# Placing the stationary halves of g at 0 or 192 bytes modulo 256 in an attention and FFN kernel

## The chip, the cores and the metric

The kernel runs on one core of a Trainium2 chip. The metric is the device time of one execution in microseconds (us). The engines are named as the profile names them: PE is TensorE's matmul stream and PEld its loading of stationary operands, DVE is VectorE, ACT is ScalarE, POOL is GpSimd, and SP is SyncE, which issues the DMAs.

## The reference

A block-sparse attention feeds a feed-forward layer with a squared ReLU, all in float32:

```python
# q, k, v: [4, 8, 768, 64]; block 32, window 16
k_sum = k.reshape(B, H, nb, 32, D).max(axis=3)
v_sum = v.reshape(B, H, nb, 32, D).mean(axis=3)
scores = concat([where(|i - j| < 16, q @ k.T / 8, -1e9), q @ k_sum.T / 8 + log(32)])
x = softmax(scores) @ concat([v, v_sum])          # -> [3072, 512]
h = x @ w_in                                      # w_in [512, 2048]
r = maximum(h, 0)
g = s * (r * r) + b
out = g @ w_out                                   # w_out [2048, 512]
```

## The kernel before

The 3072 rows are worked in 12 chunks `c` of 256 rows (three for each batch). For each chunk the attention makes `x` transposed, split into an upper and a lower part (`xh`, `xl`, type float32r), and the feed-forward layer runs over 16 steps `f` of 128 hidden columns. Two steps make a pair `q`, so a chunk has pairs 0 to 7. Products are made from halves: a number is split into an upper half that float32r holds and the rest, and lower times upper, upper times lower and upper times upper are summed.

**`hidden`** (L460) makes a step's hidden values: 12 matmuls of 256 columns into `ph`, with a slice of `wh` or `wl` stationary and a slice of `xh` or `xl` moving. **`activate`** and **`scaled`** turn `ph` into `g` in a tile `r`, for two steps at once. **`upper_rows`** (tile `gh`, a CAST at L219 on DVE or a copy at L221 on ACT) and **`lower_rows`** (tile `gl`, L492 on DVE) split it. **`project`** (L504) multiplies: for each of the two 128-row blocks `t` of the chunk there are three matmuls of 512 columns into `po[c, t]`. There the g half is stationary (a slice of 128 columns, 512 bytes) and the output weights are moving (2048 bytes). `evict` copies `po` to SBUF and stores it.

The tiles lie in SBUF at addresses that the pools give. Of those that PE reads here, every slice of `wh` and `wl` starts at 0 bytes modulo 256, and every slice of `xh` and `xl` at 192. Before the change so do all slices of `gh` and `gl`: each name has four buffers of 2048 bytes, and a slice lies at a multiple of 512 from its buffer's start. A tile pool gives a new tile a buffer of its own name; the first instruction that writes it waits until the last readers of the buffer's former tile have ended. Engines run their instructions in the order of the program; the order is fixed by hand, so the change cannot move an instruction.

From chunk 3 on the order is regular: PE does four steps of `hidden`, then four of `project` (24 matmuls, first an even pair's twelve and then an odd pair's), with the next chunk's attention in between. Before that, `FIRST_ORDER` lists every call by a letter and numbers. Those that matter here are `H` (`hidden`), `J` (`activate`), `G` (`scaled`), `a` (`upper_rows`), `b` (`lower_rows`), `P` (`project`), `X` and `y` (`xh`, `xl` of a chunk), `S` (`scores`), and `O` (`evict`). A star moves the work to the other engine. Its last line and a half is

```python
"V2.3 G1.7* V2.1 X2.0 P0.14 y2.0 P0.15 X2.2 a1.7 y2.2 S3.2.0 S3.2.1 S3.0.0 S3.0.1 b1.7 O0.0 S3.3.0 S3.3.1 "
"O0.1* S3.1.0 S3.1.1 P1.11 b1.6"
```

after which come the exponentials of chunk 3 (`masked`, L323 on DVE, and `exps`, L336 on ACT), `hidden(2, 0)` and so on. There `a1.7` is the CAST to `gh` of chunk 1's pair 7 on DVE, `P0.15` is the last projection of chunk 0, and `P1.11` is the last that reads pair 5 of chunk 1. PSUM banks are shared too: `scores(3, 0)` writes the banks from which `y2.0` and `y2.2` read, and `hidden(2, 0)` writes a bank from which the masks of chunk 3's heads 2 and 3 read.

Of the kernel before, what the change touches and what calls it, by code (L numbers as in the profile page):

```python
# [11 lines left out]
F32 = mybir.dt.float32  # L12
F32R = mybir.dt.float32r
# [6 lines left out]
P = 128  # L20
# [9 lines left out]
T = NSUB * SUB  # L30
# [14 lines left out]
def windowed_attention_then_relu2_ffn(ctx, tc, qk, vwin, kt, vt, kq, vrow, wp, out):  # L45
# [8 lines left out]
    p2 = ctx.enter_context(tc.tile_pool(name="p2", bufs=2))  # L54
# [162 lines left out]
    def copy(by_dve, out_, in_):  # L217
        if by_dve:
            nc.vector.tensor_copy(out_, in_)  # L219
        else:  # L220
            nc.scalar.copy(out_, in_)  # L221
# [254 lines left out]
    def scaled(c, q, other=False):  # L476
# [3 lines left out]
        else:  # L480
            (nc.vector if other else nc.gpsimd).tensor_scalar(g, g, s_col, b_col, ALU.mult, ALU.add)  # L481

    def upper_rows(c, q, other=False):
        g = gg[c, q]
        gh = p2.tile([P, 2 * T], F32R, name="gh", bufs=4)
        copy(not other, gh, g)
        gg[c, q] = g, gh

    def lower_rows(c, q):
        g, gh = gg[c, q]  # L490
        gl = p2.tile([P, 2 * T], F32R, name="gl", bufs=4)
        nc.vector.tensor_tensor(gl, g, gh.bitcast(F32), ALU.subtract)  # L492
        gg[c, q] = gh, gl

# [52 lines left out]
    def of(fn, *more):  # L547
# [9 lines left out]
        "Ai": of(scale_weights, "in"), "Ao": of(scale_weights, "out"), "A": of(scale_weights, "both"),  # L557
        "Bi": of(convert_weights, "in"), "Bo": of(convert_weights, "out"), "D": of(convert_weights, "both"),
        "Y": hidden_part, "H": hidden, "J": activate, "G": scaled, "a": upper_rows, "b": lower_rows,
        "P": project, "O": evict, "h": upper_weights, "l": lower_weights,  # L560
    }
# [58 lines left out]
    for i in range(NF, NC * NF):  # L620
        c, f = divmod(i, NF)

        then(i - i % 4, HID, hidden, c, f)
        if f % 2:
            for stage_of in (activate, scaled, upper_rows, lower_rows):
                then(i, CHAIN, stage_of, c, f // 2)
        then((i + 4) | 3, PROJ, project, c, f)
        if f == NF - 1:
            for t in range(T // P):
                then((i + 4) | 3, EVICT, evict, c, t)  # L630
# [60 lines left out]
```

## Time and profile before

| | |
|---|---|
| median of 3 runs (lowest to highest) | 610.86 us (609.92 to 611.22) |
| profiled execution | 609.99 us, span 608.3 us |
| granted TensorE clock | 1.000 |
| PE busy | 597.9 us (98%) |
| DVE, ACT, POOL busy | 418.8, 276.3, 140.2 us |
| bytes moved by DMA | 66.41 MB |

The span runs from the first to the last instruction of the program; what lies around it is 1.7 us of the profiled execution's time. A matmul's recorded length includes its way through the array, so that matmuls overlap in the records. The pace of PE is read from start to start.

### The profile page before, as it was taken

The page shows a single profiled execution, that of the slowest core. Times are in us where ns is not written, and L with a number is a line of the kernel's source. Part 1 is how long each engine was busy: PE and PEld are TensorE (multiplying, and loading weights), DVE is VectorE, ACT ScalarE, POOL GpSimd, SP SyncE. Part 2 cuts the span into 40 slices and gives each one's busy share as a digit, 9 for nine tenths or more (in the row PEclk, how much of TensorE's full clock was granted, in tenths as well). Part 3 has the DMA queues.
Part 4 walks back from the last instruction along what each step waited for, and adds up shares of the span by engine and source line. Part 5 has one row for each costly group of instructions (what it writes and reads, how often), then busy time and mean ns, then how long its engine had stood idle before and what let it go on. Part 6 is the DMA issues. An engine that isn't in the chain of part 4 may idle for free.

```text
span 608.3 us, 13522 instructions
## 1 busy us (share of the span) xinstructions
PE 597.9 (98%) x5240; PEld 539.2 (89%) x5240; DVE 418.8 (69%) x1126; ACT 276.3 (45%) x712; POOL 140.2 (23%) x275
## 2 busy tenths in 40 slices
PE   7999999999999999999999999999999999999997
PEld 6798999899889998999999899999998998899896
DVE  6999997789489368668758748847848927832211
ACT  5999998262352262263154244235235236223221
POOL 4421012211511411412141411331141151141110
PEclk9999999999999999999999999999999999999999
DMA  8998713026205016103503211600710500200000
GB/s 340 398 400 359 283 71 113 13 93 158 103 3 186 1 45 226 57 20 105 171 20 102 86 45 56 227 18 16 221 60 1 187 9 11 87 1 1 36 1 35
DMA packets 26993, 66.41 MB, mean 109 GB/s; under 512 B 3824, under 2 KB 3824, under 8 KB 26928
## 3 DMA queue, kind: packets, MB, share of 16 engines
q1 hardware_dynamic: 26928, 65.54, 30.5%
q8 instruction: 41, 0.67, 0.4%
q14 instruction: 24, 0.20, 0.1%
HBM read 59.09 MB, written 6.29 MB: 107 GB/s over the span
## 4 chain that ended last, share of the span: by engine, by line
PE 88%; DVE 4%; ACT 3%; DMA 2%; issue 1%; SPq 1%; POOL 0%; POOLq 0%; ACTq 0%; DVEq 0%
PE po L504 41%; PE ph L460 39%; PE pav L417 4%; PE ps L301 3%; ACT pr L336 2%; DVE pT L368 2%; DMA wraw<-in_wp_dram 1%; DMA vsum<-vmean 1%; DVE pr L346 1%; PE pt L379 1%; DVE gl L492 1%; SPq L180 0%; POOL vw L263 0%; PE ph L441 0%; SPq L240 0%
## 5 line engine op out<-in xcount | busy, mean ns | idle before, releaser
L481 POOL TENSOR_SCALAR r<-r,sb_col 128x512 f32<-128x512 f32 x85 | 69.9, 822 | 384.7 <-ACT r L474 234.6
L504 PE MATMUL po<-wh,gh 128*128 128x512 f32 x384 | 151.3, 394 | 0.0
L504 PE MATMUL po<-wh,gl 128*128 128x512 f32 x384 | 150.7, 393 | 0.0
L504 PE MATMUL po<-wl,gh 128*128 128x512 f32 x384 | 150.5, 392 | 0.0
L468 ACT ACTIVATE r<-ph 128x512 f32<-128x512 f32 x93 | 55.4, 596 | 198.8 <-PE ph L460 158.4
L219 DVE CAST gh<-r 128x512 fp32r<-128x512 f32 x88 | 38.1, 433 | 133.4 <-POOL r L481 132.4
L368 DVE STREAM_TRANSPOSE pT<-pr 32x256 f32<-32x256 f32 x288 | 125.5, 436 | 4.1
L460 PE MATMUL ph<-xh,wl 128*128 128x256 f32 x760 | 118.5, 278 | 0.0
L460 PE MATMUL ph<-xl,wh 128*128 128x256 f32 x760 | 117.3, 276 | 0.0
L460 PE MATMUL ph<-xh,wh 128*128 128x256 f32 x760 | 117.1, 276 | 0.0
L460 PEld LDWEIGHTS ph<-xh,wl 128*128 128x128 f32 x760 | 104.5, 188 | 5.1 <-DVE wl L144 0.2
L460 PEld LDWEIGHTS ph<-xl,wh 128*128 128x128 f32 x760 | 101.0, 188 | 0.0
L460 PEld LDWEIGHTS ph<-xh,wh 128*128 128x128 f32 x760 | 100.3, 188 | 0.0
L504 PEld LDWEIGHTS po<-wh,gl 128*128 128x128 f32 x384 | 72.1, 188 | 15.2 <-issue 1.0
L504 PEld LDWEIGHTS po<-wh,gh 128*128 128x128 f32 x384 | 72.2, 188 | 14.6
L504 PEld LDWEIGHTS po<-wl,gh 128*128 128x128 f32 x384 | 72.1, 188 | 14.3
L336 ACT ACTIVATE pr<-pr,mn 128x120 f32<-128x120 f32 x176 | 66.9, 383 | 23.2 <-DVE mn L323 23.1
L492 DVE TENSOR_TENSOR gl<-r,gh 128x512 fp32r<-128x512 f32 x96 | 69.6, 725 | 3.8 <-ACT gh L221 1.0
L474 ACT ACTIVATE r<-r 128x512 f32<-128x512 f32 x92 | 58.2, 633 | 5.8 <-DVE r L470 2.9
L263 POOL COPY vw<-vsum 24x256 f32<-24x256 f32 x88 | 47.1, 568 | 35.7 <-DMA vsum<-vmean 21.9
L221 ACT COPY o<-po 128x512 f32<-128x512 f32 x23 | 13.5, 587 | 45.8 <-PE po L504 44.7
L346 DVE TENSOR_TENSOR pr<-pr,rs 128x480 f32<-128x480 f32 x48 | 32.5, 676 | 2.4 <-ACT pr L336 0.5
(88 smaller groups left out, 483.0 us busy)
## 6 DMA issues: line engine op xcount, KB each, us to landing
wraw<-in_wp_dram SPq DMA_DIRECT2D x32, 512.0 KB
qk<-in_qk_dram SPq DMA_DIRECT2D x44, 369.0 KB
vw<-in_vwin_dram SPq DMA_DIRECT2D x48, 256.0 KB
out_dram<-o SPq DMA_DIRECT2D x24, 256.0 KB
kraw<-in_kt_dram SPq DMA_DIRECT2D x12, 384.0 KB
vraw<-in_vt_dram SPq DMA_DIRECT2D x12, 252.0 KB
kq<-in_kq_dram SPq DMA_DIRECT2D x4, 512.0 KB
vraw<-in_vt_dram SPq DMA_DIRECT2D x6, 264.0 KB
```

What stands on the lines that cost most here:

```text
L219: nc.vector.tensor_copy(out_, in_)
L263: nc.gpsimd.tensor_copy(vw_t[c, p][WIN:KR, e], vsum[bi][WIN : WIN + NB, 2 * p + e, :].unsqueeze(1).to_broadcast([NB, NSUB, D]),)
L336: nc.scalar.activation(pr, pr, AF.Exp, bias=mn_of[c, p][:, n : n + 1], scale=-1.0, accum_out=sm_of[c, p][:, n : n + 1])
L346: nc.vector.tensor_tensor(pr, pr, rs.unsqueeze(2).to_broadcast([P, 4, KR]), ALU.mult)
L368: nc.vector.transpose(to[BLOCK * k : BLOCK * (k + 1), :, rows], src)
L417: nc.tensor.matmul(oi, vw[:KR, e, i, :], pi[:KR], start=True, stop=True)
L460: nc.tensor.matmul(ph, w[:, kc * P : (kc + 1) * P], x[:, kc], start=(n == 0), stop=(n == len(terms) - 1))
L468: nc.scalar.activation(r, ph, AF.Relu)
L474: nc.scalar.activation(r, r, AF.Square)
L481: (nc.vector if other else nc.gpsimd).tensor_scalar(g, g, s_col, b_col, ALU.mult, ALU.add)
L492: nc.vector.tensor_tensor(gl, g, gh.bitcast(F32), ALU.subtract)
L504: nc.tensor.matmul(po[c, t], a[:, t * P : (t + 1) * P], w[:, 512:], start=(f == 0 and n == 0), stop=(f == NF - 1 and n == len(terms) - 1),)
```

## The change

The halves get two names each, `gha` and `ghb`, `gla` and `glb`, with two buffers each. In chunks 2 to 11 an even pair uses b and an odd pair a; in chunks 0 and 1 it is the other way round. A small tile `gap` (two buffers of 32 bytes) is put between the a buffers and the b buffers, so that a slices lie at 192 bytes modulo 256, as before, and b slices at 0. What lies behind them moves up by 64 bytes: `vhalf`, `vmean`, `qk` and `vw`. All of the rest stays where it was.

```diff
+    def half_name(name, c, q):
+
+        return name + "ba"[(q + (c < 2)) % 2]
+
     def upper_rows(c, q, other=False):
         g = gg[c, q]
-        gh = p2.tile([P, 2 * T], F32R, name="gh", bufs=4)
+        gh = p2.tile([P, 2 * T], F32R, name=half_name("gh", c, q), bufs=2)
         copy(not other, gh, g)
         gg[c, q] = g, gh
 
     def lower_rows(c, q):
         g, gh = gg[c, q]
-        gl = p2.tile([P, 2 * T], F32R, name="gl", bufs=4)
+        gl = p2.tile([P, 2 * T], F32R, name=half_name("gl", c, q), bufs=2)
+        if (c, q) == (0, 0):
+            p2.tile([P, 8], F32, name="gap")
         nc.vector.tensor_tensor(gl, g, gh.bitcast(F32), ALU.subtract)
         gg[c, q] = gh, gl
```

The instructions and their order are the same on every engine. What differs is which earlier reader some instructions wait for. The one place where that waits for a much later reader is DVE's `a1.7`. Before, its buffer was one that had long been read. With two buffers for each name the odd pairs of chunks 0 and 1 share two: one is held by pair 5 of chunk 1 until `P1.11`, which comes later, so `a1.7` takes that of pair 7 of chunk 0, which `P0.15` reads. DVE there before:

```order
L433 TENSOR_TENSOR xl_1745<-pav_1710,xh_1737 128x512 [waits Activation_49]
L219 CAST gh_1754<-r_1707 128x512 [waits DVE_49]
L433 TENSOR_TENSOR xl_1745<-pav_1696,xh_1737 128x512 [waits Activation_49]
L492 TENSOR_TENSOR gl_1777<-r_1707,gh_1754 128x512 [waits DVE_49]
L219 COPY o_1790<-po_847 128x512 [waits PE_49]
L492 TENSOR_TENSOR gl_1807<-r_1683,gh_1705 128x512
L323 ISA pr_1809,mn_1811<-ps_1757,mask_first_90 128x120 [waits PE_49]
```

and after (the rows are `y2.0`, `a1.7`, `y2.2`, `b1.7`, the copy of `O0.1*`, `b1.6` and the first mask of chunk 3):

```order
L433 TENSOR_TENSOR xl_1746<-pav_1711,xh_1738 128x512 [waits Activation_49]
L219 CAST ghb_1755<-r_1708 128x512 [waits DVE_49,PE_49]
L433 TENSOR_TENSOR xl_1746<-pav_1697,xh_1738 128x512 [waits Activation_49]
L498 TENSOR_TENSOR glb_1778<-r_1708,ghb_1755 128x512 [waits DVE_49]
L219 COPY o_1791<-po_848 128x512
L498 TENSOR_TENSOR gla_1808<-r_1684,gha_1706 128x512
L323 ISA pr_1810,mn_1812<-ps_1758,mask_first_90 128x120 [waits PE_49]
```

The wait for PE moved from the copy to the CAST, three instructions earlier, and it is for the same matmul: the last of `P0.15`. PE's part that depends on these rows, after the change:

```order
L301 MATMUL ps_1768<-qk_1049 64x120 [waits DVE_49,Pool_49]
L301 MATMUL ps_1768<-qk_1049 64x120
L301 MATMUL ps_1769<-qk_1049 64x120 [waits DVE_49]
...
L510 MATMUL po_897<-wh_1258,ghb_1587 128x512
L460 MATMUL ph_1854<-xh_1738,wl_443 128x256 [waits DVE_49,PE_49,Activation_49]
```

The third row waits for `y2.2`, the last for the mask that reads its bank last; both waits stand there before the change too.

## The prediction

> **What bounds the kernel now.** I read the page's head first, then the chain that ended last.
>
> ```profile
> span 608.3 us, 13522 instructions
> PE 597.9 (98%) x5240; PEld 539.2 (89%) x5240; DVE 418.8 (69%) x1126; ACT 276.3 (45%) x712; POOL 140.2 (23%) x275
> PE 88%; DVE 4%; ACT 3%; DMA 2%; issue 1%; SPq 1%; POOL 0%; POOLq 0%; ACTq 0%; DVEq 0%
> ```
>
> PE carries 88% of the chain at 98% busy, so a change of its pace counts almost everywhere. The 4% of DVE and 3% of ACT are where it does not. The same chain in order of time, from 100 to 180 us, shows where they are:
>
> ```profile
> 117.44 2.97 PE po L504 x12
> 120.41 1.40 PE ps L301 x48
> 121.84 0.28 DVE pr L323
> 122.16 4.43 ACT pr L336 x23
> ...
> 153.09 3.55 DMA vsum<-vmean
> ...
> 163.20 1.47 POOL vw L263 x2
> 164.72 1.61 PE pav L417 x46
> ```
>
> From 120.4 to 164.7 us the end is set by another line of work: chunk 3's masks on DVE, its exponentials on ACT, its normalizing and turning on DVE among the work of chunk 2, the block sums, their DMA, POOL's copies, and only then PE. The loads of PE's stationary operands show that PE really waits there:
>
> ```profile
> 162.07 0.80 PEld L417 LDWEIGHTS pav<-pT,vw 120*64 120x64 f32 x16
> 163.91 0.19 PEld L417 LDWEIGHTS pav<-pT,vw 120*64 120x64 f32 x2 [1.05 <-POOL vw L263]
> 164.72 1.47 PEld L417 LDWEIGHTS pav<-pT,vw 120*64 120x64 f32 x46 [0.62 <-POOL vw L263]
> ```
>
> The change touches this chain at its beginning, and PE's pace outside it. These are the two terms.
>
> **Term one: `a1.7` waits for `P0.15`.** The rows of PE, ACT and DVE around it, from the timeline before:
>
> ```profile
> 119.33 0.39 PE L504 MATMUL po<-wh,gh 128*128 128x512 f32 x1
> 120.02 0.40 PE L504 MATMUL po<-wh,gh 128*128 128x512 f32 x1
> 120.34 1.87 PE L301 MATMUL ps<-qk 64*64 64x120 f32 x64
> 123.63 0.28 PE L460 MATMUL ph<-xh,wl 128*128 128x256 f32 x1
> 119.76 0.59 ACT L221 COPY o<-po 128x512 f32<-128x512 f32 x1 [1.19 <-PE po L504]
> 118.72 0.42 DVE L219 CAST gh<-r 128x512 fp32r<-128x512 f32 x1
> 119.05 0.68 DVE L433 TENSOR_TENSOR xl<-pav,xh 128x512 fp32r<-128x512 f32 x1
> 119.65 0.68 DVE L492 TENSOR_TENSOR gl<-r,gh 128x512 fp32r<-128x512 f32 x1
> 120.45 0.69 DVE L219 COPY o<-po 128x512 f32<-128x512 f32 x1
> 121.06 0.68 DVE L492 TENSOR_TENSOR gl<-r,gh 128x512 fp32r<-128x512 f32 x1
> 121.84 0.28 DVE L323 CUSTOM_DVE_ANT_0 pr<-ps,mask_first 128x120 f32<-128x120 f32 x1
> 123.26 0.08 DVE L323 DVE_READ_ACCUMULATOR2_ANT mn<- 128x1 f32 x1
> ```
>
> ACT's copy of the first row block starts 0.43 us after the start of that block's last matmul (119.76 after 119.33), and DVE's copy of the second also 0.43 us after (120.45 after 120.02). So the end of `P0.15` is seen at 120.45, and that is when the CAST can start, instead of at 118.72. Behind it on DVE everything waits in order: `y2.2` 0.33 us later at 120.78 (the step of the rows above), `b1.7` 0.60 later at 121.38, the copy 0.60 later at 121.98, since its own wait is then over, `b1.6` 0.61 later at 122.59, and the first mask 0.60 to 0.78 later, at 123.19 to 123.37. It stood at 121.84: 1.35 to 1.53 us late. The least that could be recovered is nothing, which leaves the CAST's own 1.73 us. I take 1.4, since the 0.78 before the mask can hold a wait for PE's scores that is over by then; 1.35 and 1.73 are the ends.
>
> On PE this shows at two places. The second bank of `scores(3, 0)`, due a good quarter into the 1.87 us from 120.34, waits for `y2.2`, which ends at 121.46 instead of 119.73: some 0.6 us. `hidden(2, 0)` waits for the read-out of the seventh mask, at 123.34 before and about 124.75 now, and stood at 123.63: PE is then 1.1 to 1.2 us late. That lateness costs nothing more: at 162.07 plus 1.2 PE is still ahead of POOL, which lets it go on at 164.72. But POOL's end is the chain from the mask, whose links are work on DVE and ACT in order, SP's issue and a DMA that follows them; I see no idle time in it to take up 1.4 us. So PE goes on at 166.1, and all later work is PE's. A gain is excluded here, since nothing starts earlier. The other waits that changed are for matmuls that ended long before. Term one: +1.4.
>
> **Term two: b slices at 0.** How fast PE streams, from its timeline (starts), and how often:
>
> ```profile
> 295.87 0.62 PE L460 MATMUL ph<-xl,wh 128*128 128x256 f32 x4
> 296.32 0.62 PE L460 MATMUL ph<-xh,wh 128*128 128x256 f32 x4
> 296.78 0.39 PE L504 MATMUL po<-wh,gl 128*128 128x512 f32 x1
> ...
> 301.35 0.39 PE L504 MATMUL po<-wh,gh 128*128 128x512 f32 x1
> 301.58 0.39 PE L504 MATMUL po<-wh,gl 128*128 128x512 f32 x1
> ...
> 302.04 0.39 PE L504 MATMUL po<-wh,gh 128*128 128x512 f32 x1
> 302.27 0.64 PE L460 MATMUL ph<-xh,wl 128*128 128x256 f32 x4
> 302.74 0.62 PE L460 MATMUL ph<-xl,wh 128*128 128x256 f32 x4
> ...
> 303.66 0.62 PE L460 MATMUL ph<-xh,wl 128*128 128x256 f32 x4
> ...
> 305.02 0.62 PE L460 MATMUL ph<-xh,wl 128*128 128x256 f32 x4
> ```
>
> the warm-up at the start,
>
> ```profile
> 8.25 0.63 PE L199 MATMUL warm<-ident 128*128 128x128 f32 x2
> 10.38 0.63 PE L199 MATMUL warm<-ident 128*128 128x128 f32 x2
> ```
>
> and the groups of the product `wh`, `gh` after 168 us, from 35 to 99.8 and from 99.8 to 120.4:
>
> ```profile
> L504 PE MATMUL po<-wh,gh 128*128 128x512 f32 x304 | 119.7, 394 | 0.0
> L504 PE MATMUL po<-wh,gh 128*128 128x512 f32 x40 | 15.8, 394 | 0.0
> L504 PE MATMUL po<-wh,gh 128*128 128x512 f32 x14 | 5.5, 395 | 0.0
> ```
>
> The 24 projections from 296.78 to 302.27 take 228.8 ns each. `hidden`'s settled pace (12 matmuls from 303.66 to 305.02) is 113.3 ns for 256 columns, so 226.7 for 512. The warm-up matmuls at the start, ten from 8.25 to 10.38, take 213 ns for four passes over 128 columns. So a projection is stretched by something, and the address of the stationary slice could be part of it. The last three rows count one of the three products in the stretches where PE is the chain: 3 x 358 = 1074 projections, of which about half, 537, read b slices.
>
> What the trace has on the address: while a projection (moving at 0) runs, the next stationary slice is loaded. That is a g slice at 192, save under the last of the 24, where it is a slice of `wl` at 0. This one takes 0.23 us (302.04 to 302.27) as the one at 301.35 does. Under the last `hidden` matmul (moving at 192) the slice is `gl` at 192 instead of a weight at 0, and that group of four takes 0.46 us (296.32 to 296.78) as the one before does 0.45. Both combinations show no effect, so I take 0.
>
> Its ends: at most the whole stretch goes, 228.8 - 213 = 15.8 ns, times 537 = 8.5 us of gain. At worst each load disturbs the stream as in the first group after a projection, 0.47 us for four where settled ones take 0.453: 4.2 ns a load, 2.3 us of loss. The shift of `qk` and `vw` by 64 bytes I put at 0: `scores` reads both operands from one tile, so their relation stays, and a load for `values` is half as long as one of g's.
>
> Here the Trainium skill speaks on both sides, and this hangs on nothing above. Its page "SBUF — State Buffer", section "Who interferes with whom", gives PE two independent read ports and says that PE never waits on anyone; by that the sum has no second term. Its page "TensorE: Matmul & The Clock Gate", section "Back-to-back issue gap", puts an isolated matmul of N columns at N/2.4 + 2.5 ns, 215.8 for 512; this trace disagrees by 13 ns. If placing at 0 brought that pace, an estimate by that page would be 7.0 us of gain in term two, a case inside the faster rival below.
>
> **Sum.** +1.4 + 0 on the profiled 609.99 gives 611.4. That run lies 0.87 below the median of the runs shown, 610.86, so I forecast 612.3. A measurement of this kernel tells about 0.2% (1.2 us) from no change.
>
> **Rivals.**
> - Faster: the load of a slice at 192 does disturb a stream that starts at 0, and at 0 it does not. For it speaks that the stretch is there and that it is larger in `project` than in `hidden`, whose two addresses differ the other way; against it the two rows above. It decides from (1.4 + 1.2)/537 = 4.9 ns a matmul, and reaches to 15.8: 609.6 down to 603.8 us, in the middle 606.7.
> - No change: the b projections fall to `hidden`'s pace, 2.1 ns each, 1.1 us in all, which pays most of the wait: 611.1 us. The small excess over 226.7 is a loss of step that a new address may end.
> - Slower still: two streams from 0 meet, 4.2 ns a load: 614.6 us. The rows against it are the same.
> - The wait costs nothing, because some link between 121.8 and 164.7 has slack that I don't see, and addresses do nothing: 610.9 us.
>
> **Chances.** Forecast 0.34 (own range 611.6 to 613.2, from the ends of term one and the scatter of the runs; some 0.10 of it lies within 0.2%), faster 0.32, no change by pace 0.18, slower still 0.11, free wait 0.05. Faster is 0.32; within 0.2% is 0.10 + 0.17 + 0.05 = 0.32; slower is 0.24 + 0.11 + 0.01 = 0.36. The range from 606.0 to 614.8 leaves out the lowest 2.2 of the 5.8 us of the faster case, 0.12, and about half of the slowest, 0.05.
>
> **What would show it.** In the profile after: `a1.7`'s CAST directly behind the end of `P0.15`, with `y2.2` and the masks late by some 1.4 us; `hidden(2, 0)` late by over a microsecond; PE let go by POOL at about 166.1. Then in a run of 24 projections the first 12 against the last 12: equal paces near 228.8 ns would confirm that the address does nothing. I am wrong if the first 12 take 224 or less, or 231 or more, each, or if the last 12 change as well, because the two halves of a run set each other's step.

## The result, and the profile after

The changed kernel takes 617.84 us (median of 4 runs, 617.14 to 618.7), the kernel before, on the same chip, 610.39 us (609.36 to 611.22). The ratio is 1.0124, with a 95% interval of 1.0102 to 1.0145: slower by some 7.5 us, where 612.3 was forecast. Two outlying executions, 3384.58 us of the kernel before and 1529.09 us of the kernel with `x` at 128 below, are in no ratio here, and the latter kernel's median is that of its other three. The page's head after:

```profile
span 616.3 us, 13522 instructions
PE 604.9 (98%) x5240; PEld 546.5 (89%) x5240; DVE 418.6 (68%) x1126; ACT 276.2 (45%) x712; POOL 138.5 (22%) x275
PE 87%; DVE 5%; ACT 3%; DMA 3%; issue 1%; SPq 1%; POOL 0%; POOLq 0%; DVEq 0%; ACTq 0%
```

The instructions are as many as before; PE is busy 7.0 us longer, and DVE's and DMA's shares of the chain are a point higher. The chain in order of time, around the stretch that PE does not set:

```profile
118.30 2.96 PE po L510 x12
121.28 0.43 DVE ghb L219
121.71 0.60 DVE xl L433
122.31 0.60 DVE glb L498
122.91 0.60 DVE o L219
123.51 0.60 DVE gla L498
...
165.75 1.47 POOL vw L263 x2
167.27 1.61 PE pav L417 x46
```

Where it went from `P0.15` directly to the scores, it now goes through the late CAST and the four instructions queued behind it on DVE. Between its two ends on PE lie 46.0 us (121.28 to 167.27), where 44.3 lay before (120.41 to 164.72). With the stretch ahead (35 us to `P0.15`'s end: 86.3 and 85.4) and the one behind (to the end of the span: 449.0 and 443.6), the 8.0 us between the two profiled spans are 0.9 + 1.7 + 5.4, in that order.

The largest part lies where nothing was to happen. The windows view from some microseconds after POOL lets PE go, for the matmuls of one line at a time (columns: window, its length, PE busy, PEld busy, granted clock, DMA share, GB/s): `hidden` before and after, then `project` before and after.

```profile
168.00:608.00 440.00, 202.66 (x1728) 202.15 (x1728) 1.00 0.21 70
170.50:616.00 445.50, 209.38 (x1728) 208.67 (x1728) 1.00 0.21 69
168.00:608.30 440.30, 215.81 (x912) 168.54 (x912) 1.00 0.21 70
170.50:616.30 445.80, 214.94 (x912) 168.56 (x912) 1.00 0.21 69
```

The projections, half of which now read b slices, gained 0.87 us. `hidden`, whose operands stand where they stood, lost 6.72 us, at the same granted clock (the attention's `values`, 0.4 us shorter, make up the rest of the 5.4). PE's timeline shows it matmul by matmul, through one run of 24 projections and the `hidden` behind it:

```profile
230.39 0.39 PE L510 MATMUL po<-wh,glb 128*128 128x512 f32 x1
...
232.88 0.39 PE L510 MATMUL po<-wh,ghb 128*128 128x512 f32 x1
233.11 0.39 PE L510 MATMUL po<-wh,gla 128*128 128x512 f32 x1
...
235.63 0.39 PE L510 MATMUL po<-wh,gha 128*128 128x512 f32 x1
235.86 0.63 PE L460 MATMUL ph<-xh,wl 128*128 128x256 f32 x4
236.33 0.63 PE L460 MATMUL ph<-xl,wh 128*128 128x256 f32 x4
...
241.04 0.64 PE L460 MATMUL ph<-xh,wh 128*128 128x256 f32 x4
241.51 0.39 PE L510 MATMUL po<-wh,glb 128*128 128x512 f32 x1
```

The twelve b projections take 230.39 to 233.11, 226.7 ns each; the twelve a, 233.11 to 235.86, 229.2. The ten groups of four from 236.33 to 241.04 take 0.471 us each, 117.8 ns a matmul. Before, `hidden` ran at 113.3.

### The profile page after: what moved, and what is told of

It reads as the page before. It is cut to its first block, busy times and chain, and to the rows that moved or that the text cites. A ratio compares the mean times of both kernels' runs of the same rounds, so it can differ in the third digit from the quotient of the medians.

```text
span 616.3 us, 13522 instructions
## 1 busy us (share of the span) xinstructions
PE 604.9 (98%) x5240; PEld 546.5 (89%) x5240; DVE 418.6 (68%) x1126; ACT 276.2 (45%) x712; POOL 138.5 (22%) x275
## 4 chain that ended last, share of the span: by engine, by line
PE 87%; DVE 5%; ACT 3%; DMA 3%; issue 1%; SPq 1%; POOL 0%; POOLq 0%; DVEq 0%; ACTq 0%
PE po L510 40%; PE ph L460 39%; PE pav L417 3%; PE ps L301 3%; ACT pr L336 2%; DVE pT L368 2%; DMA wraw<-in_wp_dram 1%; DMA vsum<-vmean 1%; PE pt L379 1%; SPq L180 1%; DMA kq<-in_kq_dram 1%; POOL vw L263 0%; DVE pr L346 0%; DVE ksum L156 0%; DVE glb L498 0%
## 5 line engine op out<-in xcount | busy, mean ns | idle before, releaser
L219 DVE CAST ghb<-r 128x512 fp32r<-128x512 f32 x43 | 18.5, 430 | 95.4 <-POOL r L481 93.6
L510 PE MATMUL po<-wh,glb 128*128 128x512 f32 x192 | 76.0, 396 | 0.0
L510 PE MATMUL po<-wl,gha 128*128 128x512 f32 x192 | 75.6, 394 | 0.0
L510 PE MATMUL po<-wh,gla 128*128 128x512 f32 x192 | 75.4, 393 | 0.0
L510 PE MATMUL po<-wl,ghb 128*128 128x512 f32 x192 | 74.8, 390 | 0.0
L510 PE MATMUL po<-wh,ghb 128*128 128x512 f32 x192 | 74.7, 389 | 0.0
L510 PE MATMUL po<-wh,gha 128*128 128x512 f32 x192 | 74.7, 389 | 0.0
L219 DVE CAST gha<-r 128x512 fp32r<-128x512 f32 x45 | 19.2, 427 | 45.9 <-POOL r L481 45.3
L510 PEld LDWEIGHTS po<-wh,gha 128*128 128x128 f32 x192 | 36.0, 188 | 8.0
L510 PEld LDWEIGHTS po<-wh,gla 128*128 128x128 f32 x192 | 36.0, 188 | 7.7
```

Source lines behind the costliest of these rows:

```text
L510: nc.tensor.matmul(po[c, t], a[:, t * P : (t + 1) * P], w[:, 512:], start=(f == 0 and n == 0), stop=(f == NF - 1 and n == len(terms) - 1),)
```

## The experiments

The timeline prints 10 ns; the trace's records hold single nanoseconds, and from them come the steps below (start to start). In the kernel before, a run of 24 at 192 goes 226, 229, 232 ns over and over (the three-step), and 231 lies, as a rule, between its last projection and the first `hidden` matmul. I call that interval the entry step. After it come five uneven `hidden` steps (118, 116, 118, 122, 119), and then 113.3 to the end of the group: `hidden` settles. In the changed kernel the b half goes 226, 227, 227; the three-step begins with the first a slice, the entry step is 226 or 227, and `hidden` never leaves 117.8. The theory from this: **the entry step decides `hidden`'s pace**, and the slices at 0 do harm only by shifting it. The rival: **placement**, that slices at 0 in the run before unsettle `hidden` by themselves.

Ratios are against the kernel before on the same chip, with 95% intervals. The kernel before has medians from 611.9 to 612.09 us beside the experiments, against 610.39 beside the changed kernel, so times of different rounds are better compared by their ratios.

**The wait alone.** The changed kernel without the gap tile: all halves at 192, the late CAST kept.

```diff
-        if (c, q) == (0, 0):
-            p2.tile([P, 8], F32, name="gap")
```

> The change without the small gap tile: two names with two buffers each, all slices of g at 192 as before. It keeps the late wait of a1.7 and nothing else. Entry theory (hidden settles at 113.3 ns or stays near 117.8 ns a matmul according to the step on which the projections before it end) and placement theory (slices of g at 0, or the tiles behind them moved by 64 bytes, slow hidden by themselves) both expect hidden at 113.3 ns and projections at 228.9 ns. The wait alone then costs 1.4 us: 611.8 us against 610.4. If the wait is free, 610.4.

612.58 us, ratio 1.0018 (1.0003 to 1.0033), 1.1 us. DVE's timeline and the chain:

```profile
120.76 0.43 DVE L219 CAST ghb<-r 128x512 fp32r<-128x512 f32 x1 [1.65 <-PE po L508]
123.50 0.28 DVE L323 CUSTOM_DVE_ANT_0 pr<-ps,mask_first 128x120 f32<-128x120 f32 x1
166.37 1.61 PE pav L417 x46
```

`P0.15` ends 0.31 us later here than before, the first mask comes 1.66 us later (121.84 before) and PE's release 1.65 (164.72). So the wait itself costs 1.35 us at the mask, and the chain behind it hands this on whole. `hidden` settles in 32 of 36 groups; the other four were entered on 226 or 227.

**The halves mixed, without the wait.** Chunks 0 and 1 take the two names by turns, so that `a1.7` finds a free buffer.

```diff
+    made = {"gh": 0, "gl": 0}
     def half_name(name, c, q):
-        return name + "ba"[(q + (c < 2)) % 2]
+        made[name] += 1
+        return name + ("ab"[(made[name] - 1) % 2] if c < 2 else "ba"[q % 2])
```

> The change with the names in chunks 0 and 1 given by turns instead of by pair, so that every buffer is reused after four pairs as before and a1.7 waits for nothing late; from chunk 2 on the places are those of the change. Both theories expect hidden near 117.8 ns from chunk 2 on. It should be 1.4 us below the changed kernel, about 616.4 us, with PE going on after the block sums some 1.4 us earlier than in the changed kernel (167.3 us).

616.55 us, ratio 1.0069 (1.0052 to 1.0085). The CAST starts at 120.35 without waiting, and `hidden` runs at 117.8 in all 36 groups (entry 226 or 227). More than half of the loss, 0.69% of 1.24%, is there without the wait. PE goes on behind POOL at 166.48, 0.79 us before the changed kernel where 1.4 was expected, mostly since `P0.15` itself ends 0.74 later here (122.02 against 121.28).

**All halves at 0**, from the kernel before; and **only the tiles behind the halves moved** by 64 bytes (`vhalf`, `vmean`, `qk`, `vw`).

```diff
+        if (c, q) == (0, 0):
+            p2.tile([P, 8], F32, name="gap")       # ahead of gh; in the second kernel behind gl
```

> The kernel before with a gap of 64 bytes ahead of g: four buffers each, all slices of g at 0. Entry theory: projections settle at 226.7 ns in both halves, end on 226 to 227, and hidden enters on the bad step: 117.8 ns. Against the changed kernel that is no wait (-1.4) and 2.2 ns less for the other half of the projections (-1.2): about 615.2 us. Placement theory: twice as many slices at 0 slow hidden more, 120 ns or more a matmul: about 622 us.

> The kernel before with the gap of 64 bytes behind g: g stays at 192 in four buffers, and only vhalf, vmean, qk and vw move, as in the change. Entry theory: hidden at 113.3 ns, 610.4 us, no difference. If the moved tiles were what slows hidden: 117.8 ns and about 616 us.

With all at 0: 615.7 us, ratio 1.0057 (1.0042 to 1.0072); every projection at 226.7 in the steady part, entry 226 or 227, `hidden` at 117.8 in all groups. Twice the slices at 0 do no more harm than half of them, which is what the entry step says. With only the rest moved: 611.37 us, ratio 0.9987 (0.9962 to 1.0012), entry 230 or more, `hidden` settled. Moving `qk` and `vw` costs nothing that shows.

**The halves swapped**: even pairs at 192 and odd at 0, so that the run ends on slices at 0.

```diff
-        return name + "ba"[(q + (c < 2)) % 2]
+        return name + "ba"[(q + 1) % 2]
```

> The change with the places swapped from chunk 2 on: even pairs at 192 and odd pairs at 0, so that a run begins at 192 and ends at 0. Chunks 0 and 1 and the late wait are as in the change. Entry theory: projections at 0 end on 226 or 227 ns, so hidden enters on the bad step: 117.8 ns, and the first matmuls at 192 are slower after an unsettled hidden (235 to 237 ns, as at 68.6 us of the changed kernel): 618 us, no better than the change. Placement theory: as the change, 617.8 us. A time near 611 us would speak against both.

619.01 us, ratio 1.0113 (1.0072 to 1.0153): entry 226 or 227, `hidden` at 117.8 throughout.

**One a projection fewer** in the changed kernel, so that a run is twelve b and eleven a; and **two fewer** in the kernel before, with nothing at 0.

```diff
         for t in range(T // P):
             for n, (a, w) in enumerate(terms):
+                if c > 1 and f % 4 == 3 and t == 1 and n == 0:     # second kernel: n < 2
+                    continue
```

> The changed kernel, with the product of the lower half left out for the second row block of the last step in each run of projections from chunk 2 on (its output lacks that small term): a run is 23 matmuls, 12 with slices at 0 and 11 at 192. All addresses are those of the changed kernel. Entry theory: the 11th matmul at 192 is the one of 231 ns, so hidden enters on the step on which it settles: 118, 116, 118, 122, 119 and then 113.3 ns. Saved: 40 runs x 0.23 us = 9.2, and some 1750 matmuls x 4.4 ns = 7.5 us: 617.8 - 16.7, about 601 us. Placement theory (slices at 0, or the moved tiles, slow hidden by themselves): hidden stays at 117.8 ns, 608.6 us.

> The kernel before, all slices at 192, with two products left out at the end of each run from chunk 2 on (lower times upper and upper times lower of the second row block in the last step; the output lacks these terms): a run is 22 matmuls. Entry theory: the 22nd is one of 226 ns, so hidden enters on the bad step and stays near 117.8 ns although nothing lies at 0: 610.4 - 40 x 0.46 + 8, about 600 us. Placement theory: hidden settles at 113.3 ns as before, 592 us.

Eleven a steps: the entry step is 230 or 231 and `hidden` settles in all 36 groups, with half of the slices at 0. The time, 606.73 us (one run, as for the next kernel), missed the entry theory's by 5.7 us. A part of it is that the shorter run lets PE catch up with POOL, for which PE now waits five times (before: twice, 1.4 us). From start to start, from 35 us on and against the changed kernel, `hidden` is 7.4 us shorter, as expected, and the projections 7.9 instead of 9.2; the attention's `values` take 2.8 us longer and its `scores` 1.0.

```profile
PE pav L417 <- POOL vw L263: 2.7, 5, 0.9
```

With 22 steps at 192 the groups alternate, with two breaks, 18 of each kind: entered on 226 or 227 they stay at 117.8; the three-step behind such a group begins elsewhere, the next entry is 231 to 236, and that one settles. The time, 599.42 us, is near the 600 expected by luck: the 600 has all groups slow, and with half of them slow the same sum gives 596. Two neighbouring groups on PE's timeline, in fours:

```profile
222.25 0.63 PE L460 MATMUL ph<-xl,wh 128*128 128x256 f32 x4
...
225.55 0.64 PE L460 MATMUL ph<-xh,wh 128*128 128x256 f32 x4
...
232.01 0.62 PE L460 MATMUL ph<-xh,wh 128*128 128x256 f32 x4
...
236.09 0.62 PE L460 MATMUL ph<-xh,wh 128*128 128x256 f32 x4
```

Seven fours in 3.30 us are 117.9 ns a matmul, nine in 4.08 are 113.3. So `hidden` is slow with nothing at 0 and fast with half at 0: placement alone is refuted. Both kernels leave work out, though, which the last pair mends.

**Other places**, looked for because a place at which `hidden` settles from any entry would beat both kernels. From the kernel before: `x` and g at 0; `x` at 128 or 64 and g at 0; g at 64 and `x` at 192.

```diff
+            if c == 0:
+                p2.tile([P, 8], F32, name="gap")            # ahead of xh: x and g at 0
...
-                prs_of[c, p // 2] = p2.tile([P, 8 * KR + 32], F32, name="pr", bufs=2)
+                prs_of[c, p // 2] = p2.tile([P, 8 * KR + 8], F32, name="pr", bufs=2)
+            if c == 0:
+                p2.tile([P, 16], F32, name="gapx")          # x at 128; with 8: x at 64
+        if (c, q) == (0, 0):
+            p2.tile([P, 16], F32, name="gap")               # with 24 for x at 64; g at 0
...
+        if (c, q) == (0, 0):
+            p2.tile([P, 16], F32, name="gap")               # g at 64, x at 192
```

> The kernel before with a gap of 64 bytes ahead of xh: all slices of x and of g at 0, where the weights are. If a stream settles from any entry when moving and stationary operand start at the same place modulo 256 (as the projections at 0 do), then hidden does too: 113.3 ns throughout, projections 226.7 ns, and the five slow matmuls at each entry (26 ns, some 46 times) go as well: 610.4 - 2.4 - 1.2, about 606.8 us. If it is the place of g that slows hidden: as all slices of g at 0, 615 us or more.

> The kernel before, with 64 bytes ahead of xh and 64 ahead of gh (pr is 96 bytes smaller to make room): x at 128 modulo 256, all g slices at 0. Entry theory without any part for x's place: projections at 226.7, so hidden is entered on 226 or 227 and stays at 117.8: 615.7 us as with x at 192. If x's place sets hidden's pace from whatever entry: 113.3 gives 609 to 610 us, 120.0 as with x at 0 gives 620 to 621 us.

> As the last, with x at 64 modulo 256 and all g slices at 0. Entry theory without any part for x's place: hidden at 117.8, 615.7 us. If x's place sets hidden's pace: 113.3 gives 609 to 610 us, 120.0 gives 620 to 621 us.

> The kernel before, with all g slices at 64 modulo 256 and x at 192. If only the place 192 brings the three-step: projections at 226.7 and hidden at 117.8, 615.7 us. If the three-step comes with any place but 0: the projections at 228.9, entry on 231, hidden settled, 611.4 us, the time of the kernel before.

| | median us | ratio (95%) | `project`, steady ns | entry ns | `hidden` ns |
|---|---|---|---|---|---|
| x 0, g 0 | 621.11 | 1.0145 (1.0127 to 1.0163) | 226.7 | 226, 227 | 120.0 |
| x 128, g 0 | 621.63 | 1.0167 (1.0142 to 1.0191) | 226.7 | 227 | 119.9 |
| x 64, g 0 | 616.40 | 1.0075 (1.0053 to 1.0097) | 226.7 | 226, 227 | 117.8 |
| x 192, g 64 | 618.15 | 1.0107 (1.0083 to 1.0132) | 233 | 229 to 236 | 113.3 or 117.8 |

None gains. `hidden` from `x` at 0, by PE's timeline:

```profile
188.11 0.64 PE L462 MATMUL ph<-xh,wh 128*128 128x256 f32 x4
188.59 0.64 PE L462 MATMUL ph<-xh,wl 128*128 128x256 f32 x4
189.07 0.64 PE L462 MATMUL ph<-xl,wh 128*128 128x256 f32 x4
189.55 0.64 PE L462 MATMUL ph<-xh,wh 128*128 128x256 f32 x4
```

0.48 us for four, 120 ns a matmul: equal addresses of the two operands, which go with the fastest `project`, go with one of the two slowest paces of `hidden`, no better than `x` at 128. As every entry in the first three rows is 226 or 227, they don't show what another entry would do there. With g at 64, which I expected to take the pace of 0 or of 192, `project` has a pace of its own, some 231 and 236 by turns; its entries of 235 or 236 (18 groups) settle, those of 229 or 230 (18 groups) don't.

**The order alone.** First g in two places without the late wait: the lower halves all at 0 (four buffers, as before), the upper ones at 0 for even and 192 for odd pairs, so that a run ends b, a, a.

```diff
-        gh = p2.tile([P, 2 * T], F32R, name="gh", bufs=4)
+        gh = p2.tile([P, 2 * T], F32R, name=half_name(c, q), bufs=2)   # gha, ghb by turns in chunks 0 and 1
+        if len(made) == 1:
+            p2.tile([P, 8], F32, name="gap")
```

> The kernel before, with gh alone in two places: at 0 for even pairs, at 192 for odd ones (by turns in chunks 0 and 1, so that nothing waits late), and gl at 0 throughout. A run of 24 then has 16 slices at 0 and ends b, a, a: its last two steps are the first two of a three-step. Entry theory (the step on which hidden begins decides its pace): the step into hidden is 229 to 232 ns, hidden settles at 113.3 in every group, and the projections need 226.7 to 228 each: 0.7 to 1.5 us under the kernel before, about 609.9 to 610.7 us on a chip where that takes 611.4. Placement theory (any b slice in the run unsettles hidden): hidden at 117.8, about 616.5 us.

616.53 us, ratio 1.0071 (1.0055 to 1.0088). My reckoning of the step was wrong: the b slices between the a pairs delay the three-step, the entry was 226 or 227, and `hidden` ran at 117.8 in all groups. That fits both theories. So the next two kernels move nothing but matmuls within a run: in this kernel an odd pair's four lower-half matmuls (b) go ahead of its eight upper-half ones (a); in the changed kernel the first a goes ahead of the last b.

```diff
+        todo = [(t, n, a, w) for t in range(T // P) for n, (a, w) in enumerate(terms)]
+        if c > 1 and f % 4 > 1:
+            waiting.extend(todo)
+            if f % 4 == 2:
+                return
+            todo = sorted(waiting, key=lambda k: k[1] > 0)
+            waiting.clear()
...
+        if c > 1 and f % 4 == 1:                                     # second kernel
+            waiting.append(todo.pop())
+        elif c > 1 and f % 4 == 2:
+            todo.insert(1, waiting.pop())
```

> The kernel of the last b, a, a run with one thing moved: from chunk 2 on, an odd pair's four matmuls of lower halves (at 0) are issued ahead of its eight of upper halves (at 192). All the work is done, at the same addresses; a run of 24 is now 16 b and then 8 a in a row. Entry theory: eight steps into a run at 192 the three-step stands at 230 to 232 ns, as after the fifth and the eleventh; hidden is entered on that and settles at 113.3 in every group, and the projections need some 228 each: 611 to 612 us where the kernel before takes 612. Placement theory (b slices in the run unsettle hidden): hidden at 117.8, 616.5 us as before the move.

> The changed kernel with one matmul moved: from chunk 2 on, the first of an odd pair (a, at 192) is issued ahead of the last of the even pair (b, at 0), so that a run of 24 is 11 b, one a, one b, 11 a. All the work is done, at the addresses of the changed kernel, with its late CAST. Entry theory: after eleven a in a row the step into hidden is 230 or 231 ns, hidden settles at 113.3, and the time is that of the changed kernel less 5.5 to 6 us, 612 to 613 us. Placement theory: hidden at 117.8 and no change, 618 us.

Sixteen b and then eight a: **610.3 us, ratio 0.9972 (0.9957 to 0.9986)**, 6.2 us under the same addresses in the other order (0.99% by the ratios), and by its ratio a little faster than the kernel before. The profiled executions don't show this last gain: behind POOL's release they take 443.4 us here and 443.6 before, with spans of 608.7 and 608.3. Its PE timeline:

```profile
231.09 0.39 PE L520 MATMUL po<-wl,gha 128*128 128x512 f32 x1
...
232.69 0.39 PE L520 MATMUL po<-wh,gha 128*128 128x512 f32 x1
232.93 0.64 PE L460 MATMUL ph<-xh,wl 128*128 128x256 f32 x4
233.40 0.62 PE L460 MATMUL ph<-xl,wh 128*128 128x256 f32 x4
233.86 0.62 PE L460 MATMUL ph<-xh,wh 128*128 128x256 f32 x4
...
237.94 0.62 PE L460 MATMUL ph<-xh,wh 128*128 128x256 f32 x4
```

The step from 232.69 to 232.93 is 231 ns, as expected, and from 233.86 on nine fours take 4.08 us: 113.3 again, in all 36 groups. Its windows row for `hidden` is the kernel before's, and the projections' is 0.67 us shorter than 215.81:

```profile
168.00:608.00 440.00, 202.63 (x1728) 202.16 (x1728) 1.00 0.21 70
168.00:608.00 440.00, 215.14 (x912) 168.45 (x912) 1.00 0.21 70
```

The changed kernel with one matmul moved: 613.72 us, ratio 1.0034 (1.002 to 1.0048), against 1.0124 without the move. Entry 230 or 231, `hidden` settled in all groups. It is a microsecond over what I expected, because behind b, a, b the a slices took a pace that I had not seen there, 233.3 ns each: from 35 us on the projections take 2.95 us more than in the changed kernel, `hidden` 7.15 less. So the entry step came out as reckoned, but not by the three-step that I reckoned it from.

Over the thirteen kernels with `x` at 192 (the one before and the changed one among them) there are 468 groups of `hidden` after 170 us. All that were entered on 229 or less stayed at 117.8, all on 231 or more settled. At 230, those behind slices at 192 settled (29) and those behind slices at 64 did not (3). So behind slices at 192 or 0 the border lies between 227 and 230, and behind slices at 64 between 230 and 235: the entry step tells in each kernel which pace follows, but its length alone is not the whole cause, and no experiment sets it by itself. Shown is that the order of the matmuls ahead changes `hidden`'s pace with every address kept.

## Why the prediction was wrong

**What bounds the kernel**: right. PE's pace counts nearly everywhere, and `hidden`'s 6.72 us went into the span almost one to one; only the stretch from the late CAST to 167.27 is another's.

**Term one**: right in place and size. DVE's timeline after, and PE's:

```profile
121.28 0.43 DVE L219 CAST ghb<-r 128x512 fp32r<-128x512 f32 x1 [1.63 <-PE po L510]
121.62 0.68 DVE L433 TENSOR_TENSOR xl<-pav,xh 128x512 fp32r<-128x512 f32 x1
124.03 0.28 DVE L323 CUSTOM_DVE_ANT_0 pr<-ps,mask_first 128x120 f32<-128x120 f32 x1
122.36 1.45 PE L301 MATMUL ps<-qk 64*64 64x120 f32 x44 [0.36 <-DVE xl L433]
125.67 0.71 PE L460 MATMUL ph<-xh,wl 128*128 128x256 f32 x4 [0.28 <-ACT pr L336]
166.46 0.33 PE L417 MATMUL pav<-pT,vw 120*64 120x64 f32 x2 [0.91 <-POOL vw L263]
```

The CAST stands behind `P0.15`, which itself ends 0.83 us later than before (121.28 against 120.45). The first mask is 2.19 us late, of which 1.36 are the wait: the low end of 1.35 to 1.73. The scores wait 0.36 where I said 0.6; `hidden(2, 0)` starts 2.04 us later, 1.21 beyond the 0.83, at the top of 1.1 to 1.2; the profile puts its wait down to an exponential on ACT, not to the mask that I named. PE goes on at 167.27 instead of the 166.1 that I gave: the 0.83 come on top, and 0.36 more was lost along the chain.

**Term two**: here it failed, in the sentence "Both combinations show no effect, so I take 0". Each of the two rows showed one load at the seam between two kinds of matmul, printed to 10 ns where the paces differ by 2 to 5. They could not show that the run ahead decides at which of two paces the *next* stage runs. I took `hidden`'s 113.3 for a property of that instruction and used it only to price the projections; the term counted 1074 projections and no `hidden` matmul. The missing term is 1728 matmuls after 168 us at 6.72 us, 3.9 ns each (4.5 less what the five uneven steps of each settled group cost), and 0.6 between 35 and 121 us, where `hidden` lost it too. The slow pace stood in my own rows: 0.47 us for the first four behind a projection is 117.5 ns each. I priced those 4.2 ns for 537 loads of g, 2.3 us; for the 1728 `hidden` matmuls that now keep this pace they come to 7.3.

The projections did what the rival **no change by pace** said: 226.7 for b slices, 0.87 us gained after 168 us and 0.21 between 35 and 121, of the 1.1 priced. **Faster** fell: it needed 224, and the steady b steps are 226 or 227, a few 225. **Slower still** asked for a loss in the projections under the loads of g, and they got quicker. **The wait costs nothing** fell with the late CAST alone, 1.1 us. Of the signs that I named, the last came nearest, "if the last 12 change as well": the a half kept its mean of 229 and changed only its phase, and it is with the phase that `hidden`'s pace goes.

The Trainium skill's page "SBUF — State Buffer", section "Who interferes with whom", lists PE's two read ports, one for the moving operand and one for loads, as independent. The prediction drew from this that the sum has no second term. The runs disagree with that: moving only the loaded slices took `project` from 228.9 to 226.7 ns (at 0) and to 233 (at 64), and the same `hidden` instructions ran at 113.3 or 117.8 after a change of order alone. The measurement decides; whether it is the ports that tie the two streams to each other, no run shows.

## What to carry to other kernels

A steady pace in a trace may be one of several that the same instructions can hold, and what runs ahead can choose among them; before taking it as a constant, look at its first steps after every seam, and at the last step ahead of them. When operands are moved, compare the pace of all stages that share the engine, not only of the stage whose operands move. Such a loss can be won back by the order of a few instructions: 6.2 us here for putting eight matmuls last, with the operands where they were.

## What the runs showed of the hardware

- `hidden`, 256 columns with a new stationary slice for each matmul: 113.3, 117.8 or 120.0 ns at granted clock 1.0. With `x` at 192 the entry step told which of the first two follows; with `x` at 0 or 128, entered on 226 or 227, it ran at 120.0 or 119.9.
- `project`, 512 columns: 226.7 with g at 0, 226/229/232 in turn at 192, 231/236 by turns at 64, and 233.3 in one mixed order.
- Left open: why the pace of PE depends on the place of the loaded slices and on what ran ahead, and why the border of the entry step is where it is. Also open is a gap between medians and traces: with all at 0 the profiled span is 5.7 us above the profiled span before, but the ratio of 1.0057 says 3.5; some 2 us of it is that the kernel before took 609.99 in its profiled execution and 611.96 beside that experiment. Likewise the ratios of the wait alone (1.1 us) and of the mix without it (4.2) make 5.3 of the 7.5, while the two profiled spans are accounted for. The run with the wait alone had four unsettled groups in its profile; unprofiled runs of the kernel before may have some too, which would narrow the ratio, but no trace here shows it.
